# A fused attention and MoE kernel whose first half is put into one written order of small pieces

## The chip, the cores and the metric

The kernel runs on one core of a Trainium2 chip. The time is device microseconds of one execution; lower is better. The kernel before took 707.45 us (median of three runs, 704.58 to 709.62). The profiled execution took 706.18 us, and the span of its trace, from its first to its last instruction, is 704.4 us. "PE" is the engine of the matrix multiplications, "DVE" the vector engine, "ACT" the scalar engine, "POOL" GpSimd and "SP" the engine that issues nearly all transfers.

## The reference

```python
scale = 1.0 / np.sqrt(D)                      # B, H, S, Ns, D = 8, 8, 512, 32, 64
scores = scale * np.matmul(x, state.transpose(0, 1, 3, 2))
a = softmax(scores)                           # over the 32 states
xread = np.matmul(a, state)
scores2 = scale * np.matmul(state, x.transpose(0, 1, 3, 2))
a2 = softmax(scores2)                         # over the 512 tokens
sread = np.matmul(a2, x)
y = np.concatenate([xread, sread], axis=2)    # 8 x 8 x 544 x 64 -> 4352 tokens x 512
h = np.maximum(y @ w_in, 0.0)                 # w_in 512 x 2048
out = h * h @ w_out                           # w_out 2048 x 512
```

Here `softmax` stands for the subtraction of the maximum, the exponential and the division by the sum. `w_in` and `w_out` arrive as 64-bit floats and are decoded to 32 bits on the chip.

## The kernel before

**What is computed in which form.** For a batch, `xread @ w_in` is `a @ (state @ w_in)`, so the kernel makes a small matrix W2 = state @ w_in for each batch (256 rows of heads and states by 2048) and multiplies the attention weights by that. The weights of the second matrix stay as they are. Products are done in two parts: every operand X is split into a rounded `hi` and a rest `lo`, and a product is hi*hi + hi*lo + lo*hi (`mm3`, L303).

**Blocks and chunks.** There are nine blocks of tokens: the 512 token rows of each of the eight batches, and a ninth of the 256 rows of `sread` of all batches. The 2048 columns of `w_in` are cut into 16 chunks of 128, called fc. `hidden.b.fc` (L638) makes the chunk of the hidden layer: six multiplications 128x512 into a tile `ph`, a square of the positive part on ACT alone (L651, L652, keys under `square` in SECOND) or on ACT and DVE (L655, L656), a `g_hi` on ACT (L657) and a `g_lo` on DVE (L662). `accumulate.b.fc` (L665) multiplies it by `w_out` into four tiles `acc`, twelve multiplications for a batch. Batches 0 and 1 are interwoven over the first 16 chunks, and their sums are stored after four and eight chunks (`keep_first`, `keep_part`) so that both can share the decoded chunks of `w_out`.

**Preparing a batch.** `start`, `load` and `prep` bring x and transpose it (L382; for batches 0 and 1 by PE with `ident`, L394, and copies on DVE or ACT, for later ones on DVE, L388). `scores` multiplies by the states. The softmax over states transposes the scores on DVE (`transposed_scores`, L409), takes the maximum, the difference, the exponential, the sum and the quotient (L434 to L451), transposes back on DVE (L449) and splits into `k_hi` and `k_lo`. `exp_s` (L412) is the softmax over tokens; `transposes` and `sread` finish it.

**Preparing weights.** `load_raw` brings a piece of `w_in` (512 KB), `decode_wi` decodes it (L316: an absolute value on ACT, a clamp on DVE or POOL, three bit operations on DVE) and writes it to memory. `prep_wo` does the same for a chunk of `w_out` and splits it (L631). `direct_w2.hb` makes W2 for batches 0 and 1 and 256 columns, `later_w2.hb.2` and `later_w2.hb.4` for batches 2 to 5, `last_w2` for 6 and 7; before the later ones `load_wf` reads the decoded `w_in` back (512 KB, L541). The results of the later ones go to memory (L584) and come back by `load_w2` (L613), which splits them on ACT and on DVE or POOL (L621, L279).

**What sets the order.** PLAN (L24) lists these steps in order. The program calls them one after another, but each engine's own order is then set by a scheduler that moves instructions by estimated times. Only instructions under `keep_in_program_order` stay: from `hidden.2.8` on (PINNED_FROM) those of PE, the loads of `w_out`, and those named under `pin` in SECOND. SECOND (L188) also says which engine does an operation that two could do. Each engine runs its instructions strictly in its order, and SP issues transfers strictly in its own. PSUM holds four `acc` tiles, two `ph` tiles and two `psb` tiles for all the rest (L253 to L255).

Of the kernel before, what the change touches and what calls it, by code (L numbers as in the profile page):

```python
# [23 lines left out]
PLAN = """  # L24
    load_raw.0 ident neg_ident start.0 load.0.1 load_states.0 load_raw.1 states.0 decode_wi.0 prep.0.0
        load_raw.2 load_wo.0 decode_wi.1 direct_w2.0 prep_wo.0 load_wo.1 decode_wi.2 start.1 load.1.1
    prep_wo.1 load_raw.3 decode_wi.3 prep.0.1 scores.0 transposed_scores.0.1 softmax.0.1 exp_s.0.1
# [3 lines left out]
    prep_wo.3 softmax.1.0 softmax.1.1 load_wo.4 accumulate.0.0
    exp_s.1.0 exp_s.1.1 direct_w2.1 hidden.0.2 hidden.0.3 transposes.0 sread.0 load_wo.5 accumulate.0.1
    hidden.1.0 decode_wi.4 load_raw.6 decode_wi.5 load_raw.7 direct_w2.2 load_wo.6 load_wo.7 accumulate.0.2
    hidden.1.1 transposes.1 prep_wo.4 decode_wi.6 load_raw.8 decode_wi.7 direct_w2.3 load_raw.9
        accumulate.0.3
    hidden.1.2 prep_wo.5 sread.1 accumulate.1.0
    hidden.1.3 prep_wo.6 prep_wo.7 load_wo.8 load_wo.9 accumulate.1.1
# [16 lines left out]
    hidden.0.13 softmax.2.0 load_n.2.0 load_part.0 accumulate.0.11
    hidden.0.14 later_w2.3.2 later_w2.3.4 load_wf.1.4 later_w2.4.2 load_w2.1.5 later_w2.4.4 accumulate.0.12
    hidden.0.15 softmax.2.1 load_n.2.1 accumulate.0.13
    hidden.1.8 transposes.2 accumulate.0.14
    hidden.1.9 load_wf.1.5 load_w2.1.6 accumulate.0.15
    hidden.1.10 sread.2 accumulate.1.8
    hidden.1.11 later_w2.5.2 later_w2.5.4 load_wf.1.6 load_w2.1.7 accumulate.1.9  # L60
    hidden.1.12 start.3 load_part.1 accumulate.1.10
# [834 lines left out]
```

## Time and profile before

| | |
|---|---|
| time of the profiled execution | 706.18 us |
| span of its trace | 704.4 us |
| median of the runs | 707.45 us |
| busy: PE, DVE, ACT, POOL | 660.6, 375.3, 334.7, 78.2 us |
| moved by transfers | 100.36 MB, 142 GB/s |
| mean granted clock of PE | 0.991 |

How to read it: an engine's busy time is the union of its instructions' spans, so a PE that is busy may still run slower than it could. A view of windows gives each engine's busy time in stretches of the span, with the number of instructions in brackets behind an x. A group line gives line, engine, operation, output<-input by tile names with their numbers left out, shapes and types, the count, then busy time and the mean of one in nanoseconds, then the idle time just before these instructions and what ended it. A line of the view of waits says who waited for whom, for how long in all, how often and at most. Lines of a timeline begin with the start and the length in us.

### The profile page before, as it was taken

How to read it: one execution, taken by the hardware profiler on the slowest of the kernel's cores; microseconds unless marked ns; L12 is line 12 of the kernel's file. 1: busy time of each engine (PE TensorE's matmuls, PEld its weight loads, DVE VectorE, ACT ScalarE, POOL GpSimd, SP SyncE). 2: the span in 40 equal slices, each digit the busy share in tenths (PEclk: the TensorE clock that was granted, in tenths of full speed). 3: DMA queues.
4: the chain of work that ended last, by engine and by line, in shares of the span. 5: the costliest groups of instructions: out<-in, count | busy, mean ns of one | idle time of the engine just before them, and what ended most of it. 6: DMA issues, size and time to landing. Idle time of an engine off the chain costs nothing.

```text
span 704.4 us, 11391 instructions
## 1 busy us (share of the span) xinstructions
PE 660.6 (94%) x4365; PEld 512.0 (73%) x4365; DVE 375.3 (53%) x691; ACT 334.7 (48%) x643; POOL 78.2 (11%) x66
## 2 busy tenths in 40 slices
PE   4668899979989999999999999999999999999997
PEld 1445666657667777887788778877887788888885
DVE  4999988667444448244924382438332733433232
ACT  2657765365623436434634464445444544444322
POOL 0302021013200003000300021002100200100000
PEclk9989999999999999999999999999999999999999
DMA  9556577895588775333533353433432223230003
GB/s 231 128 208 187 174 235 273 192 371 175 186 247 237 207 217 163 76 106 121 176 72 108 121 174 70 116 104 97 143 120 76 86 79 120 60 91 30 31 1 89
DMA packets 120710, 100.36 MB, mean 142 GB/s; under 512 B 68048, under 2 KB 96976, under 8 KB 120656
## 3 DMA queue, kind: packets, MB, share of 16 engines
q1 hardware_dynamic: 120512, 99.51, 47.8%
q8 instruction: 34, 0.56, 0.3%
q10 hardware_dynamic: 144, 0.13, 0.1%
q14 instruction: 20, 0.16, 0.1%
HBM read 65.54 MB, written 34.08 MB: 141 GB/s over the span
## 4 chain that ended last, share of the span: by engine, by line
PE 71%; DVE 9%; DMA 9%; SPq 4%; ACT 3%; issue 2%; POOL 0%; DVEq 0%; ACTq 0%
PE acc L309 43%; PE ph L309 22%; DMA wi_raw<-in_moe_w_in_dram 3%; SPq L376 2%; DMA w_d<-w2o 2%; DMA wo_raw<-in_moe_w_out_dram 2%; PE w2ps L341 1%; PE w2ps L338 1%; PE pt L472 1%; DVE wf L329 1%; DMA xp<-in_x_dram 1%; PE st L338 1%; DMA win_f<-wf 1%; DMA wf<-win_f 1%; DVE wf L330 1%
## 5 line engine op out<-in xcount | busy, mean ns | idle before, releaser
L309 PE MATMUL acc<-wo,g_hi 128*128 128x512 f32 x1086 | 338.6, 397 | 8.0 <-ACT wo L278 3.0
L309 PEld LDWEIGHTS acc<-wo,g_hi 128*128 128x128 f32 x1086 | 202.1, 190 | 62.1 <-issue 4.5
L309 PE MATMUL acc<-wo,g_lo 128*128 128x512 f32 x543 | 208.0, 392 | 0.0
L309 PE MATMUL ph<-k_hi,w 128*128 128x512 f32 x512 | 180.8, 395 | 5.8 <-DVE g_lo L662 2.7
L662 DVE TENSOR_TENSOR g_lo<-ph,g_hi 128x512 fp32r<-128x512 f32 (+1 forms) x140 | 91.4, 655 | 135.8 <-ACT g_hi L657 133.8
L309 PEld LDWEIGHTS ph<-k_hi,w 128*128 128x128 f32 x512 | 96.3, 189 | 31.6 <-DVE g_lo L662 4.9
L309 PEld LDWEIGHTS acc<-wo,g_lo 128*128 128x128 f32 x543 | 102.4, 189 | 23.1 <-issue 1.2
L657 ACT CAST g_hi<-ph 128x512 fp32r<-128x512 f32 (+1 forms) x144 | 81.2, 565 | 49.7 <-DVE ph L656 42.4
L309 PE MATMUL ph<-k_lo,w 128*128 128x512 f32 x256 | 100.6, 393 | 0.1
L655 ACT ACTIVATE r<-ph 128x512 f32<-128x512 f32 (+1 forms) x77 | 43.7, 568 | 107.3 <-PE ph L309 107.0
L656 DVE SCALAR_TENSOR_TENSOR ph<-ph,r 128x512 f32<-128x512 f32 (+1 forms) x77 | 50.6, 657 | 82.8 <-ACT r L655 82.5
L651 ACT ACTIVATE ph<-ph 128x512 f32<-128x512 f32 (+1 forms) x67 | 38.0, 567 | 98.1 <-PE ph L309 98.1
L309 PEld LDWEIGHTS ph<-k_lo,w 128*128 128x128 f32 x256 | 48.4, 189 | 10.5 <-DVE k_lo L279 0.5
L279 POOL TENSOR_TENSOR w<-w_f,w 128x512 fp32r<-128x512 f32 x18 | 24.1, 1339 | 283.4 <-ACT w L278 283.4
L652 ACT ACTIVATE ph<-ph 128x512 f32<-128x512 f32 (+1 forms) x67 | 38.1, 569 | 1.4
L341 PE MATMUL w2ps<-wf,sT 64*32 64x256 f32 x960 | 35.8, 390 | 0.7 <-ACT srd L494 0.7
L278 ACT CAST w<-w_f 128x512 fp32r<-128x512 f32 x40 | 24.5, 614 | 5.0 <-DMA w_f<-w_d 5.0
L388 DVE STREAM_TRANSPOSE xT<-xp 128x512 f32<-128x512 f32 x24 | 16.0, 693 | 18.7 <-PE st L341 9.5
L338 PE MATMUL w2ps<-wf,sT 64*32 64x256 f32 x64 | 20.1, 395 | 5.9 <-DVE wf L330 4.0
L309 PE MATMUL ph<-sr_hi,s 128*128 128x256 f32 x128 | 25.5, 282 | 0.0
L279 POOL TENSOR_TENSOR s<-sf,s 128x512 fp32r<-128x512 f32 x8 | 10.3, 1292 | 128.8 <-ACT s L278 128.8
L309 PEld LDWEIGHTS ph<-sr_hi,s 128*128 128x128 f32 x128 | 21.0, 191 | 0.6
(94 smaller groups left out, 557.3 us busy)
## 6 DMA issues: line engine op xcount, KB each, us to landing
w_d<-w2o SPq DMA_DIRECT2D x40, 256.0 KB, 4.5
w_f<-w_d SPq DMA_DIRECT2D x40, 256.0 KB, 3.1
wi_raw<-in_moe_w_in_dram SPq DMA_DIRECT2D x16, 512.0 KB, 5.1
wo_raw<-in_moe_w_out_dram SPq DMA_DIRECT2D x16, 512.0 KB, 6.4
wf<-win_f SPq DMA_DIRECT2D x16, 512.0 KB, 4.3
w<-w2a_d SPq DMA_DIRECT2D x16, 512.0 KB, 3.3
out_dram<-o SPq DMA_DIRECT2D x31, 256.0 KB, 3.0
xp<-in_x_dram SPq DMA_DIRECT2D x96, 64.0 KB, 2.8
```

Source lines behind the costliest of these rows:

```text
L278: nc.scalar.copy(hi, src)
L279: pick(key, nc.gpsimd, nc.vector).tensor_sub(lo, src, hi.bitcast(F32))
L309: m = nc.tensor.matmul(ps, l, r, start=first and i == 0, stop=last and i == len(seq) - 1, skip_group_check=skip)
L338: in_order(call())
L341: tc.keep_in_program_order(call())
L388: nc.vector.transpose(xT[:, c], self.xp[g][:, c])
L651: nc.scalar.activation(ph, ph, AF.Relu)
L652: nc.scalar.activation(ph, ph, AF.Square)
L655: nc.scalar.activation(r, ph, AF.Relu)
L656: nc.vector.scalar_tensor_tensor(ph, ph, 0.0, r, ALU.max, ALU.mult)
L657: nc.scalar.copy(ghi, ph)
L662: nc.vector.tensor_sub(glo, ph, ghi.bitcast(F32))
```

## The change

The change rewrites the order of the work up to the fourth batch and a few operations with it.

- Every engine's instructions up to `hidden.3.0` (LOOSE_FROM) are kept in program order, by a wrapper around the engines (`InOrder`). The scheduler moves none of them. From there on PLAN and the scheduler are as before, but for `load_wf.2.3`.
- Steps are generators with a `yield` between their instructions. A name in PLAN that is repeated runs one piece of its step each time, so PLAN orders single instructions. `accumulate` of batches 0 and 1 now does all `hi` products first and, as a piece of its own, the `lo` products.
- The softmax over states of batches 0 and 1 is done from PE transposes: `keep_s` copies the scores on ACT to SBUF, PE transposes them into PSUM (`pst`), DVE takes maximum and difference from there, PE transposes the result back (`pa`), and the split reads that. x of these batches is loaded in rows of 1 KB and loaded again later (`load_n`, tile `xr`) for `sread`; `exp_s` of these batches comes later.
- For the first 512 of the 2048 columns (`hb` 0 and 1, NOW = 2) W2 of all eight batches is made in a row from the decoded `w_in` while it is still in SBUF, and four of the sixteen reads `load_wf` are gone. The products of `hb` 0 for batches 2 to 7 use the two `ph` tiles.
- SECOND moves operations between engines. Over the whole program, in counts: squares on ACT alone 62 to 81 (those shared with DVE 66 to 47, chunks of 512 tokens); copies of W2 out of PSUM on DVE 16 to 7; splits of `w_out` on POOL 7 to 13; clamps on POOL 2 to 8; corrections on PE (`neg_ident`, L293) 10 to 4.

Lines of the changed kernel below are those of its own file; nearly all its instructions are issued on line 317, so tile names tell them apart.

```diff
 PLAN = """
-    hidden.0.1 prep_wo.2 prep.1.0 prep.1.1 scores.1 transposed_scores.1.0 load_raw.5 transposed_scores.1.1
-        load_raw.4
+    hidden.0.1 hidden.0.1 hidden.0.1 accumulate.0.0 second_w2.1 hidden.0.1 hidden.0.1 softmax.1.0 prep_wo.1
+        prep_wo.1 hidden.0.1 softmax.1.1 softmax.1.1 softmax.1.1 prep_wo.1 prep_wo.1 softmax.1.0 softmax.1.0
...
+LOOSE_FROM = "hidden.3.0"
 PINNED_FROM = "hidden.2.8"
...
+class InOrder:
+    def __init__(self, engine, tc, held):
+        self.engine, self.tc, self.held = engine, tc, held
+    def __getattr__(self, name):
+        call = getattr(self.engine, name)
+        def issue(*args, **kw):
+            op = call(*args, **kw)
+            if self.held:
+                self.tc.keep_in_program_order(op)
+            return op
+        return issue
...
-    nc = tc.nc
+    held = ["start"]
+    nc = Engines(tc.nc, tc, held)
...
         def transposed_scores(self, g):
             b = self.b
+            if b < NT:
+                pool, tag = (ps_acc, "acc") if b == 0 else (ps_b, "psb")
+                self.sp[g] = pool.tile([P, S], F32, tag=tag, name=f"pst{b}_{g}")
+                for k in range(KC):
+                    nc.tensor.transpose(self.sp[g][:, ts(k, P)], self.e_all[:, g, ts(k, P)], ident)
+                return
...
+            if b < NT:
+                pool, tag = (ps_acc, "acc") if b == 0 else (ps_b, "psb")
+                pa = pool.tile([P, S], F32, tag=tag, name=f"pa{b}_{g}")
+                for k in range(KC):
+                    nc.tensor.transpose(pa[:, ts(k, P)], sp[:, ts(k, P)], ident)
+                yield
+                nc.scalar.copy(khi[:, g], pa)
+                yield
+                nc.vector.tensor_sub(klo[:, g], pa, khi[:, g].bitcast(F32))
+                return
...
     def two_w2(hb, b0, last):
         w = (wf.pop(hb) if last else wf[hb]).bitcast(F32)
-        ps = [ps_b.tile([P, 2, HB], F32, tag="psb", name=f"w2ps{hb}_{b0}_{g}") for g in range(G)]
+        pool, tag = (ps_h, "ph") if hb == 0 < b0 else (ps_b, "psb")
+        ps = [pool.tile([P, 2, HB], F32, tag=tag, name=f"w2ps{hb}_{b0}_{g}") for g in range(G)]
...
     def direct_w2(hb):
-        ps = two_w2(hb, 0, True)
+        ps = two_w2(hb, 0, hb >= NOW)
...
     def later_w2(hb, b0):
-        keep_w2(hb, b0, two_w2(hb, b0, b0 == 4))
+        yield from keep_w2(hb, b0, two_w2(hb, b0, b0 == 4 and hb >= NOW))
...
         ghi, glo = g
+        if blk < NX:
+            for i in range(nt // P):
+                for r in range(2):
+                    nc.tensor.matmul(acc[i], ghi[:, ts(i, P)], wo[fc][:, r], start=first and r == 0, stop=False)
+            yield
+            for i in range(nt // P):
+                nc.tensor.matmul(acc[i], glo[:, ts(i, P)], wo[fc][:, 0], start=False, stop=last)
+            return
...
+        if begun[k] is None or left[k] == 0:
+            for _ in begun[k] or ():
+                pass
+            done.add(k)
+        else:
+            next(begun[k], None)
```

**Two places where the instructions move.** On DVE, behind the first batch's softmax and ahead of its first `g_lo`. Before (`dec` and `wf` are pieces of `w_out` and `w_in` being decoded, `nb2`, `s2` and `r2` are small tiles of `exp_s` of batch 0, `xT1` is x of batch 1):

```order
L430 TENSOR_SCALAR r20_1_283<-s20_1_281 128x1
L329 SCALAR_TENSOR_TENSOR dec0_191<-wo_raw0_154,dec0_191 128x512
L431 RECIPROCAL r20_1_283<-r20_1_283 128x1
L323 TENSOR_SCALAR wf1_202<-wf1_202 128x512
L330 SCALAR_TENSOR_TENSOR dec0_191<-wo_raw0_154,dec0_191 128x512
...
L430 TENSOR_SCALAR r20_0_308<-s20_0_306 128x1
L326 TENSOR_SCALAR wf1_202<-wf1_202 128x512 x2
L431 RECIPROCAL r20_0_308<-r20_0_308 128x1
L329 SCALAR_TENSOR_TENSOR wf1_202<-wi_raw3_230,wf1_202 128x512
L329 SCALAR_TENSOR_TENSOR wf1_202<-wi_raw2_152,wf1_202 128x512
L287 COPY xT1_1_364<-px1_1_1_371 128x512
```

In the changed kernel (`pst1` and `pa0` are PE's transposes for batches 1 and 0, `m11` the maxima):

```order
L317 TENSOR_TENSOR k_lo0_120<-pa0_0_330,k_hi0_119 128x512
L317 TENSOR_TENSOR k_lo0_120<-pa0_1_337,k_hi0_119 128x512
L317 TENSOR_SCALAR dec0_328<-dec0_328 128x512
L317 TENSOR_SCALAR wf1_242<-wf1_242 128x512
L317 SCALAR_TENSOR_TENSOR dec0_328<-wo_raw0_182,dec0_328 128x512
...
L317 SCALAR_TENSOR_TENSOR wf1_242<-wi_raw3_244,wf1_242 128x512
L317 TENSOR_REDUCE m11_1_422<-pst1_1_410 128x16
...
L317 TENSOR_TENSOR sp1_1_421<-pst1_1_410,m11_1_422 128x512
```

The small operations of `exp_s` and the copies of `xT1` have left this stretch of DVE, and batch 1's softmax stands directly behind batch 0's.

On SP, where the loads for the second half of the first 16 chunks stand. Before (`w2_d` is W2 in memory, written from `w2o`; `w2_f` is its reload; `wi_raw` and `wo_raw` are raw weights, `win_f` the decoded `w_in`):

```order
L628 DMA wo_raw11_1068<-in_moe_w_out_dram 128x1024
L537 DMA win_f6_83<-wf6_1105 128x512
L525 DMA wi_raw14_1112<-in_moe_w_in_dram 128x2x512
L620 DMA w2_f0_4_1206<-w2_d4_89 128x512
L628 DMA wo_raw12_1210<-in_moe_w_out_dram 128x1024
L537 DMA win_f6_83<-wf6_1105 128x512
L525 DMA wi_raw15_1146<-in_moe_w_in_dram 128x2x512
```

In the changed kernel:

```order
L317 DMA wo_raw8_1020<-in_moe_w_out_dram 128x1024
L317 DMA w2_d4_89<-w2o4_0_0_1055 128x2x256
L317 DMA wi_raw11_1118<-in_moe_w_in_dram 128x2x512
L317 DMA w2_d4_89<-w2o4_0_1_1094 128x2x256
L317 DMA win_f5_82<-wf5_1018 128x512
L317 DMA win_f6_83<-wf6_1078 128x512
L317 DMA wi_raw13_1143<-in_moe_w_in_dram 128x2x512
L317 DMA wo_raw10_1147<-in_moe_w_out_dram 128x1024
L317 DMA part_d0_101<-po0_0_1167 128x512
L317 DMA part_d0_101<-po0_1_1170 128x512
L317 DMA w2_f0_4_1177<-w2_d4_89 128x512
```

Raw pieces of `w_in` now stand later in the queue beside the reload of W2: pieces 11 and 13 where 14 and 15 stood, each behind writes of results that ACT or DVE must first have made.

More of the change, by code (lines that the diff above doesn't have):

```diff
@@ L31 @@
[L31 to L37, printed above, removed]
@@ L54 @@
[L54 to L61, printed above, removed]
@@ new lines @@
+    hidden.2.10 accumulate.2.9 load_n.2.1 transposes.2 transposes.2 hidden.2.10 hidden.2.10 hidden.2.10
+        load_w2.3.1 transposes.2 transposes.2 hidden.2.10 softmax.3.0 load_n.2.0
+    hidden.2.11 hidden.2.11 load_w2.2.6 hidden.2.11 hidden.2.11 hidden.2.10 load_w2.3.1 hidden.2.11
+        hidden.2.11 load_w2.2.7 later_w2.5.4 load_w2.2.7 later_w2.5.4 load_w2.2.7 accumulate.2.10
+        softmax.3.0 load_wf.2.2 sread.2 sread.2 sread.2 later_w2.5.4 sread.2 sread.2
+    hidden.2.12 later_w2.5.4 hidden.2.12 hidden.2.12
@@ new lines @@
+    hidden.2.13 hidden.2.12 hidden.2.12 hidden.2.12 exp_s.3.1 later_w2.5.4 exp_s.3.0 transposes.3
+        transposes.3 transposes.3 transposes.3 load_w2.3.0 accumulate.1.15 load_n.3.0 hidden.2.13
+        hidden.2.13 hidden.2.13 hidden.2.13 hidden.2.13 softmax.3.0 softmax.3.0 accumulate.2.11 load_w2.3.0
+        softmax.3.0 softmax.3.0 softmax.3.0 softmax.3.0
+    hidden.2.14 load_n.3.1
+    hidden.2.15 hidden.2.15 hidden.2.15 hidden.2.15 hidden.2.15 hidden.2.15 later_w2.7.4 later_w2.7.4
+        later_w2.7.4 later_w2.7.4 accumulate.2.12 load_w2.3.1 hidden.2.14 hidden.2.14 hidden.2.14
+        hidden.2.14 load_w2.3.0 hidden.2.14 later_w2.7.4 sread.3 sread.3 sread.3 accumulate.2.13 sread.3
+        sread.3
@@ L620, in load_w2 @@
         nc.sync.dma_start(raw, w2_d[hb][b])
-        split(*weights[b, hb], raw, f"w2_lo.{b}.{hb}")
+        yield
+        yield from split(*weights[b, hb], raw, f"w2_lo.{b}.{hb}")
     wo = {}
@@ L752, in step_hidden @@
             ks[blk] = att[blk].k
-        gs[blk, fc] = hidden(blk, fc, tok[blk])
+        yield from hidden(blk, fc, tok[blk])
     def step_accumulate(blk, fc):
@@ L799, in tile_attn_moe @@
             key("sread", b), lambda b: att[b].sread(), b,
-            after=[key("transposes", b)] + [key("load_n", b, g) for g in range(G)] * (not early),
+            after=[key("transposes", b)] + [key("load_n", b, g) for g in range(G)],
         )
@@ L855, in tile_attn_moe @@
             step(key("accumulate", blk, fc), step_accumulate, blk, fc, after=needs)
[L857 to L859 removed]
+    plan = PLAN.split()
+    left = {k: plan.count(k) for k in steps}
+    done, begun = set(), {}
+    for k in plan:
+        if k == LOOSE_FROM:
+            held.clear()
         if k == PINNED_FROM:
             pinned.append(k)
[L862 to L864 removed]
+        if k not in begun:
+            f, args, after = steps[k]
+            assert done.issuperset(after), f"{k} needs {set(after) - done}"
+            begun[k] = f(*args)
+        left[k] -= 1
+        if begun[k] is None or left[k] == 0:
+            for _ in begun[k] or ():
+                pass
+            done.add(k)
+        else:
+            next(begun[k], None)
     assert done == set(steps), set(steps) - done
```

452 lines of the change are left out of this document (317 added, 135 removed), and 3 rows, old and new, of the table SECOND.

## The prediction

> **What bounds the kernel now.** I read the slices of the page first.
>
> ```profile
> span 704.4 us, 11391 instructions
> PE   4668899979989999999999999999999999999997
> DVE  4999988667444448244924382438332733433232
> ```
>
> PE is full from about the tenth slice of 17.6 us on; before that it isn't, and DVE is full just there. To see the stretches, I cut the span at four instructions of PE: the first multiplication of `hidden.0.0`, `hidden.0.4`, `hidden.0.12` and `hidden.3.0`, found by counting `ph` multiplications in the order (288 without the corrections stand before the last).
>
> ```profile
> 26.38 1.22 PE L309 MATMUL ph<-k_hi,w 128*128 128x512 f32 x2 [0.42 <-ACT k_hi L278]
> 87.02 0.39 PE L309 MATMUL ph<-k_hi,w 128*128 128x512 f32 x1
> 154.15 0.39 PE L309 MATMUL ph<-k_hi,w 128*128 128x512 f32 x1
> 299.29 0.39 PE L309 MATMUL ph<-k_hi,w 128*128 128x512 f32 x1
> ```
>
> ```profile
> core 0: us, PE busy (x) PEld busy (x) DVE busy (x) ACT busy (x) POOL busy (x), PEclk, DMA share, GB/s
> 0.00:26.40 26.40, 11.51 (x74) 5.01 (x74) 16.43 (x33) 8.86 (x17) 4.26 (x9) 1.00 1.02 233
> 26.40:87.00 60.60, 48.03 (x391) 33.17 (x392) 58.35 (x123) 41.42 (x87) 9.64 (x7) 0.92 0.49 164
> 87.00:154.10 67.10, 59.32 (x467) 42.87 (x467) 48.22 (x85) 35.97 (x68) 8.61 (x5) 1.00 0.84 264
> 154.10:299.30 145.20, 142.57 (x1138) 105.41 (x1138) 78.04 (x142) 69.04 (x130) 19.49 (x16) 1.00 0.66 192
> 299.30:704.40 405.10, 399.22 (x2300) 325.49 (x2298) 174.26 (x313) 179.43 (x343) 36.16 (x29) 1.00 0.32 95
> ```
>
> From 26.4 to 87.0 us DVE is busy 58.35 of 60.6 us (96%), and hardly ever waits:
>
> ```profile
> DVE r L430 <- ACT e L421: 1.0, 1, 1.0
> DVE wf L323 <- ACT wf L322: 0.7, 1, 0.7
> DVE w L577 <- ACT w L572: 0.3, 1, 0.3
> ```
>
> So this stretch is DVE's. The next is mixed: no engine is full, and the transfers are at 0.84. From 154 us on PE sets the time (142.57 of 145.2, then 399.22 of 405.1), and no order of the others can shorten that by more than its few idle microseconds. The change has its room ahead of 154 us.
>
> **The end, from `hidden.3.0`.** PLAN and scheduler are the same but for one read. I take 405.1 us as it is. With the 1.8 us that the execution (706.18) is longer than its span, the sum needs only the time of `hidden.3.0`, now 299.3.
>
> **What leaves DVE.**
>
> ```profile
> L656 DVE SCALAR_TENSOR_TENSOR ph<-ph,r 128x512 f32<-128x512 f32 x66 | 45.8, 695 | 67.2 <-ACT r L655 66.9
> L287 DVE COPY w2o<-w2ps 128x512 f32<-128x512 f32 x16 | 10.8, 680 | 4.2 <-PE w2ps L341 4.1
> L279 DVE TENSOR_TENSOR wo<-dec,wo 128x512 fp32r<-128x512 f32 x9 | 6.3, 705 | 1.4 <-ACT wo L278 1.3
> L409 DVE STREAM_TRANSPOSE sp<-st 128x512 f32<-128x512 f32 x16 | 11.1, 700 | 3.6 <-PE st L341 3.6
> L655 ACT ACTIVATE r<-ph 128x512 f32<-128x512 f32 x66 | 39.5, 599 | 89.2 <-PE ph L309 89.0
> L652 ACT ACTIVATE ph<-ph 128x512 f32<-128x512 f32 x62 | 36.3, 585 | 1.2
> ```
>
> Nineteen squares fewer (19 x 0.695 = 13.2 us), nine copies of W2 (6.1), six splits of `w_out` (4.2) and eight transposes of the softmax (5.6) are 29 us; smaller moves in both directions roughly cancel. On ACT the squares cost 19 x (2 x 0.585 - 0.599) = 10.9 us. The copies of W2 and the four `keep_s` are thirteen more operations of that length, 7.6 us. ACT has the room: it is busy 41.42 of 60.6 us where DVE is full.
>
> What the sum needs is how much stands ahead of `hidden.0.12`. Now DVE has run 33 + 123 + 85 = 241 instructions by then, 123.0 us, 0.510 us each. In the new order 205 stand ahead of that chunk's `g_lo`: `exp_s`, `transposes` and `sread` of batches 0 and 1 come later too. 205 x 0.510 = 104.6 us.
>
> **What POOL takes on.**
>
> ```profile
> L446 POOL TENSOR_TENSOR sp<-sp,s 128x512 f32<-128x512 f32 x11 | 12.3, 1122 | 47.4 <-DVE s L445 46.9 <-PE ph L309 0.5
> L279 POOL TENSOR_TENSOR wo<-dec,wo 128x512 fp32r<-128x512 f32 x7 | 9.8, 1396 | 38.4 <-ACT wo L278 36.5 <-PE ph L309 1.9
> L323 POOL TENSOR_SCALAR wf<-wf 128x512 f32<-128x512 f32 x2 | 4.3, 2156 | 5.2 <-DMA win_f<-wf 3.8 <-ACT wf L322 1.4
> ```
>
> Ahead of `hidden.0.12` the order has 8 clamps (8 x 2.156), 10 splits of `w_out` (10 x 1.396), 3 products of the softmax (3 x 1.122) and a split of about 1.4 us: 36 us where POOL now has 4.26 + 9.64 + 8.61 = 22.5. It stays far from full. A clamp on POOL is a wait added for DVE: the shift of the same piece stands in DVE's queue, with the rest of that queue behind it. On DVE an operation of that size takes 0.42 us (row L326 below), on POOL 2.156, so eight exposed clamps would cost 8 x 1.7 = 14 us. The order puts other pieces of DVE's work ahead of the shift (between the clamp of `dec0` and its shift, batch 0's last products and `k_lo`), and I count nothing, with 14 us as the bound. But DVE's decoding is slower beside POOL:
>
> ```profile
> 31.68 1.40 POOL L279 TENSOR_TENSOR wo<-dec,wo 128x512 fp32r<-128x512 f32 x1 [3.99 <-ACT wo L278]
> 31.95 1.68 DVE L329 SCALAR_TENSOR_TENSOR wf<-wi_raw,wf 128x512 uint32<-128x512 uint32 x1
> L329 DVE SCALAR_TENSOR_TENSOR wf<-wi_raw,wf 128x512 uint32<-128x512 uint32 x16 | 11.8, 745 | 0.2
> L330 DVE SCALAR_TENSOR_TENSOR wf<-wi_raw,wf 128x512 uint32<-128x512 uint32 x16 | 10.8, 682 | 0.2
> L326 DVE TENSOR_SCALAR wf<-wf 128x512 uint32<-128x512 uint32 x16 | 8.5, 537 | 0.8 <-POOL wf L323 0.6
> L326 DVE TENSOR_SCALAR dec<-dec 128x512 uint32<-128x512 uint32 x16 | 6.7, 419 | 0.1
> ```
>
> The one at 31.95 took 1.68 us instead of 0.68. POOL's 13.5 us more are about ten instructions; the bounds are 0 and ten times 1.0 us. The means show 16 x (0.063 + 0.118) = 2.9 us over these two kinds, so I take 3 us. [...]
>
> **What PE gains and loses.**
>
> ```profile
> 300.81 2.72 PE acc L309 x12
> 278.05 1.09 PE pt L472 x8
> 91.90 0.40 PE L338 MATMUL w2ps<-wf,sT 64*32 64x256 f32 x1
> 92.92 0.50 PE L293 MATMUL ph<-g_hi,neg_ident 128*128 128x512 f32 x1
> 85.85 1.01 PE L341 MATMUL pr<-xn,eT 128*32 128x64 f32 x59
> ```
>
> A large multiplication is 0.227 us in a row, a transpose 0.136, a W2 product of two batches (91.90 to 92.92) 1.02. The transposes of two softmaxes are 32 x 0.136 = 4.4 us more, six corrections fewer about 1.4 us less: 3.0 us more in all. Ahead of `hidden.0.12` the order also has 16 more `acc` (3.6) and three more W2 products (3.1), and 64 `pr` (about 2.0) and 8 `pt` (1.1) fewer: 6.6 us more done. So `hidden.0.12` to `hidden.3.0` keeps 145.2 - (6.6 - 3.0) = 141.6 us.
>
> **When `hidden.0.12` comes.** DVE stands idle 154.1 - 123.0 = 31.1 us ahead of it. Keeping every idle microsecond, DVE gives 104.6 + 3 + 31.1 = 138.7. PE, with its 118.9 busy us, 6.6 more, and only the idle 14.9 us ahead of 26.4, gives 140.4. The lower end is DVE at its 96% behind 26.4: 26.4 + (107.6 - 16.4) / 0.963 = 121. The upper end is 154 (nothing gained), or beyond it (the slower rival). The new order brings DVE, ACT and PE close together, so each will wait for the others at times; I take the side where the idle time stays, **140**.
>
> Sum: 140 + 141.6 + 405.1 + 1.8 = **688.5 us**, 17.7 under the profiled execution; on the median of the runs, 1.3 us higher, it would be 689.8.
>
> **Edits costed at nothing.** Four reads fewer:
>
> ```profile
> PE w2ps L338 <- DMA wf<-win_f: 1.6, 3, 1.1
> ```
>
> PE waits 1.6 us in all for such reads, so no more than that can come of them directly. Fewer and larger pieces of x: transfers are at 1.02 in the first 26.4 us, so if they stayed as long, `hidden.0.0` would come no earlier; the sum doesn't use it. The W2 products of `hb` 0 in the `ph` tiles stand ahead of `hidden.0.1`, which must wait until ACT and DVE have emptied them (two copies of 0.59 us a pair, the length of the ACT operations above): covered by the softmax of batch 1, which needs those engines anyway; 3 x 1.2 us if that cover is gone.
>
> The clock row is 0.92 between 26.4 and 87.0 us: 0.08 x 60.6 = 4.8 us of full speed lost. [...]
>
> **The rivals.** (a) *A larger gain.* PE and DVE really interlock: `hidden.0.12` at 128, between 121 and 140, giving 676.5. For it: DVE waits 2.0 us in 60 now. Against: three engines near their limit. (b) *Transfers keep the date.* `hidden.0.12` needs W2 that was loaded, decoded, multiplied, written and read back, and the share of 0.84 shows a busy queue; SP's new order puts raw pieces behind writes. Then it stays at 154.1, only 3.6 us of PE's work are saved: 702.6. Against: the share is 0.49 up to 87 us, 30 us to spare. (c) *Slower: loads hold ACT.*
>
> ```profile
> ACT wf L322 <- DMA wi_raw<-in_moe_w_in_dram: 17.9, 10, 3.1
> ACT dec L322 <- DMA wo_raw<-in_moe_w_out_dram: 13.3, 9, 4.5
> ```
>
> ACT's 178 instructions ahead of `hidden.0.12`, at (8.86 + 41.42 + 35.97) / 172 = 0.501 us, are 89 us, with 5 us for the first load 94. Thirty-one of them open a decoding and wait for a load, with squares queued behind, and PE waits for those. At the 1.64 us that a wait has now, that is 145 in all, near the forecast. From 2.05 us on (157.7) the gain is gone. At 2.5 us, half as long again, it is 171.7, and the kernel takes 720.2.
>
> **How the numbers follow.** Chances: forecast 0.48 (own range 681 to 697), (a) 0.22, (b) 0.16, (c) 0.14. A measurement can tell about 1% here, 7 us. Forecast and (a) are faster by more, with a little of (b): 0.72; same 0.14; slower 0.14. The range from 670 to 708 leaves out (c) and the far end of (a).
>
> **What would show it.** `hidden.0.12` near 140 and `hidden.3.0` near 282, with the 405 us behind it unchanged; some 205 DVE instructions ahead of the former; DVE no longer at 96% up to 87 us. The prediction is wrong if ACT's waits for loads grow past 60 us, if the stretch behind `hidden.3.0` changes by more than 3 us, or if PE is cut up by short waits all over the first 150 us.

## The result, and the profile after

The changed kernel takes **682.02 us** (median of 4 runs, 680.75 to 684.21) where the kernel before took 707.87 beside it (4 runs, 704.58 to 709.62): a ratio of 0.9643, with a 95% interval from 0.96 to 0.9687. Forecast were 688.5 us, range 670 to 708. The profiled execution took 684.21 us, its span 682.3.

The slices of the page, as they answer to those of before:

```profile
span 682.3 us, 11470 instructions
PE   4899997999999997999999999999999999999997
DVE  5899997877433445438443743465234614323232
PEclk9899999999999999899999999999999999999999
```

PE is now full from the third slice on (17.1 us each), but for the 7th and the 16th, and DVE is still full in slices 3 to 6. The same four first multiplications cut the span (in the third row two are printed together, and the chunk's own is the second, at 133.3):

```profile
26.07 0.50 PE L317 MATMUL ph<-k_hi,w 128*128 128x512 f32 x1
66.11 0.47 PE L317 MATMUL ph<-k_hi,w 128*128 128x512 f32 x1
133.10 0.62 PE L317 MATMUL ph<-k_hi,w 128*128 128x512 f32 x2
277.29 0.39 PE L317 MATMUL ph<-k_hi,w 128*128 128x512 f32 x1
```

`hidden.0.4` comes at 66.1 instead of 87.0 us, `hidden.0.12` at 133.3 instead of 154.1, `hidden.3.0` at 277.3 instead of 299.3. So 20.9 of the 22.0 us are won ahead of `hidden.0.4`; the stretch from there to `hidden.0.12` takes 67.2 us as it took 67.1, and the end 405.0 instead of 405.1. Busy time by stretch, after:

```profile
core 0: us, PE busy (x) PEld busy (x) DVE busy (x) ACT busy (x) POOL busy (x), PEclk, DMA share, GB/s
0.00:26.10 26.10, 15.36 (x212) 11.64 (x212) 15.80 (x29) 14.80 (x30) 5.58 (x9) 0.93 0.93 285
26.10:66.10 40.00, 38.87 (x336) 26.90 (x330) 38.76 (x71) 33.23 (x66) 13.19 (x9) 1.00 0.78 249
66.10:133.30 67.20, 61.69 (x424) 46.48 (x425) 57.95 (x104) 44.12 (x83) 15.22 (x10) 0.97 0.83 253
133.30:277.30 144.00, 139.48 (x1162) 105.81 (x1161) 74.69 (x135) 79.91 (x152) 24.62 (x20) 0.98 0.60 176
277.30:682.30 405.00, 399.18 (x2300) 325.54 (x2298) 174.07 (x312) 179.40 (x343) 36.16 (x29) 1.00 0.34 101
```

Read DVE's column against the one of before. Up to `hidden.0.4` it was busy 16.43 + 58.35 = 74.8 us and idle 12.2; now it is busy 15.80 + 38.76 = 54.6 and idle 11.5. Its idle time has hardly changed: the 20.9 us are 20.2 us of DVE's work that no longer stand there. Half of that has not gone away. In the next stretch DVE does 57.95 us instead of 48.22, and that stretch is no longer for it, since DVE was idle 18.9 us there and now only 9.2.

The loads that hold ACT (rival c) were 31.2 us of waits before; now, up to `hidden.0.12`:

```profile
ACT wf L317 <- DMA wi_raw<-in_moe_w_in_dram: 6.9, 5, 2.5
ACT dec L317 <- DMA wo_raw<-in_moe_w_out_dram: 1.1, 2, 0.6
```

Two single waits behind a reloaded W2 remain, the first two rows on ACT, the third PE's wait behind the second of them:

```profile
115.85 0.62 ACT L317 CAST w<-w_f 128x512 fp32r<-128x512 f32 x1 [4.47 <-DMA w_f<-w_d]
268.43 0.62 ACT L317 CAST w<-w_f 128x512 fp32r<-128x512 f32 x1 [1.93 <-DMA w_f<-w_d]
270.69 1.94 PE L317 MATMUL pr<-xr,eT 128*32 128x64 f32 x64 [4.17 <-ACT w2o L317]
```

What made the first load late is in SP's queue: its read of W2 waits for the write of W2, and that stands behind eight reads of x which take SP 8.08 us. The second read of W2 stands directly behind eight more (the last two rows).

```profile
99.20 8.08 SPq L317 DMA_DIRECT2D xp<-in_x_dram  x8
108.52 0.40 SPq L317 DMA_DIRECT2D w_d<-w2o  x1
111.95 0.33 SPq L317 DMA_DIRECT2D w_f<-w_d  x1
...
257.07 7.71 SPq L317 DMA_DIRECT2D xp<-in_x_dram  x8
264.88 0.57 SPq L317 DMA_DIRECT2D w_f<-w_d  x1
```

### The profile page after: what moved, and what is told of

It is laid out like the page before. It is cut to its first block, busy times and chain, and to the rows that moved or that the text cites. A ratio compares the mean times of both kernels' runs of the same rounds, so it can differ in the third digit from the quotient of the medians.

```text
span 682.3 us, 11470 instructions
## 1 busy us (share of the span) xinstructions
PE 654.6 (96%) x4423; PEld 516.4 (76%) x4423; DVE 361.3 (53%) x648; ACT 351.5 (52%) x672; POOL 94.8 (14%) x76
## 4 chain that ended last, share of the span: by engine, by line
PE 73%; DVE 13%; DMA 7%; ACT 4%; issue 2%; SPq 1%; POOL 0%; DVEq 0%; ACTq 0%; POOLq 0%
PE acc L317 44%; PE ph L317 22%; DVE wf L317 3%; PE w2ps L317 2%; DVE dec L317 2%; DMA xn<-in_x_dram 2%; DMA w_f<-w_d 2%; DVE g_lo L317 2%; PE pr L317 1%; DVE s L317 1%; DMA w_d<-w2o 1%; DMA wi_raw<-in_moe_w_in_dram 1%; PE st L317 1%; DVE sp L317 1%; DVE m L317 1%
## 5 line engine op out<-in xcount | busy, mean ns | idle before, releaser
L317 PE MATMUL acc<-wo,g_hi 128*128 128x512 f32 x1090 | 326.1, 395 | 0.0
L317 PE MATMUL acc<-wo,g_lo 128*128 128x512 f32 x545 | 197.8, 392 | 0.5 <-DVE g_lo L317 0.3
L317 ACT ACTIVATE ph<-ph 128x512 f32<-128x512 f32 (+1 forms) x172 | 98.4, 572 | 104.1 <-PE ph L317 101.7
L317 ACT ACTIVATE r<-ph 128x512 f32<-128x512 f32 (+1 forms) x58 | 32.3, 558 | 90.9 <-PE ph L317 90.8
L317 DVE SCALAR_TENSOR_TENSOR ph<-ph,r 128x512 f32<-128x512 f32 (+1 forms) x58 | 37.4, 644 | 73.1 <-ACT r L317 72.9
L317 POOL TENSOR_TENSOR w<-w_f,w 128x512 fp32r<-128x512 f32 x21 | 27.3, 1303 | 205.9 <-ACT w L317 202.7
L317 POOL TENSOR_TENSOR s<-sf,s 128x512 fp32r<-128x512 f32 x8 | 10.3, 1292 | 128.8 <-ACT s L317 128.8
L317 PE MATMUL w2ps<-wf,sT 64*32 64x256 f32 x768 | 26.9, 382 | 0.1
L317 DVE SCALAR_TENSOR_TENSOR wf<-wi_raw,wf 128x512 uint32<-128x512 uint32 x32 | 25.4, 795 | 0.9
L317 ACT COPY w2o<-w2ps 128x512 f32<-128x512 f32 x33 | 18.7, 591 | 12.6 <-PE w2ps L317 11.4
L317 DVE SCALAR_TENSOR_TENSOR dec<-wo_raw,dec 128x512 uint32<-128x512 uint32 x32 | 24.1, 754 | 0.6
```

Of the source, the lines that this page charges most:

```text
L317: op = call(*args, **kw)
```

## The experiments

My theory at the outset: DVE's amount of work sets the time up to `hidden.0.12`, and the work that left it makes the gain. The rival: the written order makes it. Each kernel ran on the same chip as the kernel before, beside it (705.93 to 707.87 us in the median there), and the ratio is to that. Dates are those of the profiled execution (which took 5.3 us more than the median for e7, 3.3 for e10, and within 2.3 of it for the others); "DVE" is its busy and its idle time ahead of `hidden.0.4`.

| kernel | median us | ratio to before (95%) | 0.4 | 0.12 | 3.0 | DVE to 0.4 |
|---|---|---|---|---|---|---|
| before | 707.87 | 1 | 87.0 | 154.1 | 299.3 | 74.8 + 12.2 |
| after | 682.02 | 0.9643 (0.96 to 0.9687) | 66.1 | 133.3 | 277.3 | 54.6 + 11.5 |
| e1_free_order | 713.19 | 1.0096 (1.0065 to 1.0126) | 93.9 | 159.0 | 304.5 | 64.8 + 29.1 |
| e2_squares_back | 688.96 | 0.9752 (0.9705 to 0.9799) | 68.7 | 134.7 | 282.3 | 56.0 + 12.7 |
| e3_new_sides_old_order | 726.78 | 1.0293 (1.0248 to 1.0338) | 85.5 | 158.3 | 316.8 | 70.5 + 15.0 |
| e4_two_stalls | 679.41 | 0.9624 (0.9577 to 0.9672) | 66.0 | 131.1 | 268.2 | 54.8 + 11.2 |
| e5_old_sides | 731.29 | 1.0315 (1.0266 to 1.0364) | 92.2 | 171.7 | 324.5 | 65.5 + 26.7 |
| e6_x4_early | 676.13 | 0.9548 (0.951 to 0.9587) | 68.5 | 133.1 | 270.3 | 54.7 + 13.8 |
| e7_hold_dve_act | 696.74 | 0.9863 (0.9816 to 0.991) | 76.5 | 146.4 | 293.5 | 56.5 + 20.0 |
| e8_hold_pe_sp | 721.99 | 1.0202 (1.0167 to 1.0236) | 93.3 | 165.1 | 314.2 | 61.7 + 31.6 |
| e9_held_to_0_4 | 703.43 | 0.9946 (0.9925 to 0.9966) | 71.4 | 149.5 | 297.6 | 59.4 + 12.0 |
| e10_dve_pad | 689.56 | 0.9766 (0.9736 to 0.9796) | 72.9 | 142.5 | 285.9 | 60.7 + 12.2 |
| e11_act_pad | 681.95 | 0.965 (0.9628 to 0.9673) | 65.2 | 131.4 | 275.7 | 54.8 + 10.4 |
| e12_clamps_back | 684.17 | 0.9692 (0.966 to 0.9725) | 66.8 | 133.5 | 277.3 | 55.1 + 11.7 |

### e1_free_order: the same operations without the written order

```diff
-LOOSE_FROM = "hidden.3.0"
+LOOSE_FROM = "load_raw.0"
```

> The changed kernel with all its operations and sides, but LOOSE_FROM is its first step, so that nothing is held and the scheduler places every instruction, as it did before the change. My theory: the gain comes from the work that has left DVE (some 29 us) and the written order only lets it be used; then the scheduler, with the same amounts on the same engines, keeps most of it: hidden.0.12 by 141 us and 682 to 690 us in all. Rival: the gain is made by the written order, since the scheduler orders by modelled durations and the loads land later than modelled; then hidden.0.12 falls back to 150 us or later and the kernel takes 697 to 708 us.

The rival is right, and beyond its range: 713.19 us, 1.0% slower than before the change. The loss, 27.2 us at `hidden.3.0`, has all arisen by `hidden.0.4` (27.8). Its first stretch, and ACT's and DVE's waits in it:

```profile
0.00:93.90 93.90, 69.10 (x559) 45.83 (x560) 64.83 (x124) 55.30 (x108) 25.54 (x22) 0.87 0.62 198
```

```profile
ACT wf L317 <- DMA wi_raw<-in_moe_w_in_dram: 9.8, 6, 4.9
ACT wo L317 <- DVE dec L317: 7.1, 4, 2.9
ACT dec L317 <- DMA wo_raw<-in_moe_w_out_dram: 4.5, 2, 3.5
ACT dec L317 <- POOL wo L317: 3.1, 4, 1.2
```

```profile
DVE wf L317 <- ACT wf L317: 6.8, 2, 5.3
DVE r L317 <- ACT e L317: 5.2, 1, 5.2
DVE g_lo L317 <- ACT g_hi L317: 4.4, 3, 2.3
DVE m L317 <- ACT e L317: 3.8, 1, 3.8
```

The scheduler does two things that the written order doesn't. It puts 124 DVE instructions ahead of `hidden.0.4` instead of 99 or 100 (10.3 us more), and it puts instructions at the head of ACT's queue whose input is not there: ACT waits 14.3 us for loads (4.5 in the changed kernel), 7.1 for DVE's decoding (0.9) and 3.1 for POOL (none), and DVE then stands idle 29.1 us instead of 11.5. (Of the rows of DVE's waits, the first was there before: 5.5 us in the changed kernel; the other three are not in its list.) Why the scheduler chose so, the rival's modelled durations, was not tried.

### e2_squares_back, e3_new_sides_old_order, e5_old_sides: the sides

In e2 the `square` row of SECOND is the one of before, in e3 the kernel before has the whole new table, in e5 the changed kernel has the whole old one. The table has the `pin` row too, so that e3 also changes what the scheduler may not move: `decode_wi.3` and `decode_wi.8` are pinned in addition, `decode_wo.2`, `exp_s.0.0` and `exp_s.0.1` no longer. Of e2's diff the first line:

```diff
-    square: 0.0 0.1 0.2 0.3 0.4 0.6 0.7 0.8 0.9 0.10 0.11 0.12 0.13 0.14 0.15 1.0 1.1 1.2 1.3 1.4 1.5 1.6
...
+    square: 0.0 0.1 0.2 0.3 0.4 0.6 0.7 0.9 0.10 0.11 0.12 0.13 1.1 1.3 1.6 1.8 1.10 2.0 2.2 2.3 2.6 2.9
```

> The changed kernel with the squares on the sides that they had before: twenty go back from ACT to DVE and ACT together, one goes to ACT. Everything else, the written order too, stays. Six of the twenty stand ahead of hidden.0.12 (6 x 0.695 = 4.2 us of DVE), thirteen net behind it. My theory (DVE's amount of work sets the date up to hidden.0.12, PE from there on): hidden.0.12 comes 3 to 5 us later, near 137 us, the stretch from there to hidden.3.0 stays within 1.5 us of 144, and the kernel takes 685 to 688 us. Rival (DVE has room in the written order, and ACT, which the squares load twice, was no worse off): hidden.0.12 stays within 1 us of 133.3 and the kernel within 1.5 us of 682.

The total lies 1 us above what I had expected of my theory, but not where I had put it: `hidden.0.12` is only 1.4 us later, and 3.4 of the 5.0 us at `hidden.3.0` arise in batch 2 (193.5 to 282.3, 88.8 us, against 191.9 to 277.3, 85.4). DVE is far from full there. What is different in the rows is that PE, full from 191.9 to 251.9 us in the changed kernel, has gaps in two of the same three pieces of 20 us here (18.70 and 19.72 busy). They make 1.6 of the 3.4 us; PE's busy time in batch 2 is another 1.6 us longer (82.84 instead of 81.23). A square by DVE sends a chunk to ACT, DVE, ACT and DVE again instead of ACT and DVE; that this longer way makes the gaps is argued from the order, not shown.

> The kernel before the change with the new table of sides (SECOND) and nothing else: its own plan, the scheduler's order, softmax of all batches by DVE's transposes. Ahead of hidden.0.12 about 15 us leave DVE (six squares 4.2, some five copies of W2 3.4, six splits of w_out 4.2, eight clamps 3.4). My theory by DVE relief: hidden.0.12 comes 8 to 14 us earlier, 140 to 146, and the kernel takes 693 to 700 us. Rival (sides alone are worth nothing without the order): within 3 us of 707, since ACT's and POOL's waits take the place of what DVE saves.

Neither: the new sides without the new order cost 21 us against the kernel before beside them (705.93). DVE's 4.3 us of relief ahead of `hidden.0.4` are there (70.45 instead of 74.78), but `hidden.0.12` comes at 158.3 and the stretch behind it takes 158.5 us instead of 145.2.

> The changed kernel in its written order with the table of sides (SECOND) of before. The first four kernels have turned my theory over: the same operations and sides under the scheduler take 713 us, and the new sides in the old order 727. New theory: the written order makes the gain, and the sides pay only in it. Then with the old sides the order alone keeps most: about 22 squares, copies and splits return to DVE ahead of hidden.0.12 (some 15 us less what waits hide), hidden.0.12 between 140 and 148, 690 to 698 us in all. Rival (order and sides were made for each other, neither is worth anything alone): 703 us or more, no better than before the change.

The rival, and beyond it: 731.29 us. The order with the old sides leaves DVE idle 26.7 us ahead of `hidden.0.4`. Where the old sides have an operation on another engine, the head of the next engine's queue waits for it, as I read these rows (in the changed kernel the first is 5.5 us, the last 1.3, and the other two are not in the lists):

```profile
DVE wf L314 <- ACT wf L314: 8.4, 3, 5.4
DVE ph L314 <- ACT r L314: 5.5, 1, 5.5
```

```profile
ACT ph L314 <- PE ph L314: 8.0, 4, 5.1
ACT w2o L314 <- PE w2ps L314: 4.0, 2, 2.6
```

So everything but the sides costs 24 us and the sides, with their pins, 21, and together they gain 26: this order and these sides were made for each other. An order fit for the old sides was not tried, and e5 holds the other edits too (the PE transposes, the early W2), so 24 us is not the order's price alone. With e1 and e3 my theory, as I had stated it, has fallen: the relief of DVE makes no gain by itself.

### e7_hold_dve_act, e8_hold_pe_sp, e9_held_to_0_4: which part of the order

In e7 only DVE and ACT are held, in e8 only PE and SP, with the other pair in the second line; in e9 `LOOSE_FROM` is `"hidden.0.4"`.

```diff
-            if self.held:
+            if self.held and self.kept:
...
-            setattr(self, name, InOrder(getattr(nc, name), tc, held))
+            setattr(self, name, InOrder(getattr(nc, name), tc, held, name in ('vector', 'scalar')))
```

> The changed kernel with the written order kept on DVE and ACT alone; PE, POOL and SP are placed by the scheduler. Theory A (the gain is the order on the two engines that are near full ahead of hidden.0.4: no instruction that waits for a late transfer stands ahead of ready ones): hidden.0.4 by 72 us, 682 to 692 us in all. Theory B (it is PE's and SP's order, what is read and multiplied first): 700 us or more.

> The counterpart: the written order kept on PE and SP alone; DVE, ACT and POOL are placed by the scheduler. Theory A (the order of DVE and ACT makes the gain): 700 us or more, hidden.0.4 later than 85 us. Theory B (PE's and SP's order makes it): hidden.0.4 by 72 us, 682 to 692 us in all. If both of these come near 682, either order leads the scheduler to the other; if both come near 710, only the order of all engines together makes the gain.

e8 is clear: with PE and SP alone held, DVE is idle 31.6 us ahead of `hidden.0.4`, and the kernel is slower than with nothing held. e7 lies between the two theories: `hidden.0.4` at 76.5, 10.5 of the 20.9 us, and 696.74 in all. Against the kernel with nothing held (e1) DVE's and ACT's order alone gains 16 us; another 15 come only when PE, POOL and SP are held with them, although PE's and SP's order alone loses 9. Against the kernel before, e7 is worth about 10 us of 26.

> The changed kernel with the written order kept only up to hidden.0.4; from there on the scheduler places everything. In e1_free_order the whole loss stood ahead of hidden.0.4 (27.8 us there, 27.2 at hidden.3.0). Theory (what the written order is worth, it is worth in the first 66 us): hidden.0.4 within 2 us of 66, from there to hidden.3.0 210 to 215 us as in all the other kernels, 681 to 687 us in all. Rival (the order is worth as much behind hidden.0.4, and the scheduler loses there what it gets early): hidden.0.4 to hidden.3.0 over 220 us, 692 us or more.

The rival. From `hidden.0.4` to `hidden.3.0` it takes 226.2 us instead of 211.2, and `hidden.0.4` itself is 5.3 us late, since the scheduler slips 15 DVE instructions of later steps in ahead of it (114 instead of 99). Work that was put off is still to be done: the scheduler, with some 9 us of DVE's work more behind `hidden.0.4` than before the change (56.93 instead of 48.22), doesn't fit it into DVE's idle time as the written order does (78.1 us to `hidden.0.12` instead of 67.2).

```profile
71.40:149.50 78.10, 65.25 (x418) 46.32 (x417) 56.93 (x101) 42.62 (x81) 16.98 (x11) 0.91 0.81 248
```

### e10_dve_pad, e11_act_pad: is DVE full, and has ACT room?

Ten operations of 128x512 that nobody needs are put at ten places between `hidden.0.0` and `hidden.0.4`; e11 has `nc.scalar.copy(srall[:, 2:], srall[:, :2])` there.

```diff
+    def pad():
+        nc.gpsimd.memset(srall[:, :2], 1.0)
+        for _ in range(10):
+            yield
+            nc.vector.tensor_sub(srall[:, 2:], srall[:, :2], srall[:, :2])
+
+    step("pad", pad)
```

> The changed kernel with ten subtractions of 128x512 (0.6 to 0.7 us each) added to DVE's written order, evenly between hidden.0.0 and hidden.0.4; they write to a tile that holds nothing yet, so no other engine waits for their results. They add 6 to 7 us to DVE. Theory (DVE, busy 38.76 of 40.0 us there, sets the time of this stretch): hidden.0.4 5.5 to 7 us later, at 71.6 to 73, and 4 to 7 us more in all, 686 to 689. Rival (PE, busy 38.87 us of the same 40.0, sets it, and DVE's work can slide into the next stretch, where it has 9 us of room): hidden.0.4 within 2 us of 66, 682 to 684 in all.

> The same with ten copies of 128x512 (0.5 to 0.6 us each) on ACT at the same places. Theory (ACT has 6.8 us of 40 left, so that squares and copies could go to it): hidden.0.4 at most 2.5 us later, and 682 to 685 us in all. Rival (in a written order each instruction that is put into a queue delays all behind it, whatever room the engine has): hidden.0.4 5 to 6 us later and 687 us or more, as much as the same work costs on DVE.

The added groups (count, then shortest, median and longest in ns), and the stretch up to `hidden.0.4`, first on DVE, then on ACT:

```profile
L317 DVE TENSOR_TENSOR srall<-srall x10: 679/681/687, 30.1 to 76.5; 128x512 f32<-128x512 f32 x10
```

```profile
0.00:72.90 72.90, 57.59 (x540) 38.68 (x540) 60.69 (x108) 47.89 (x94) 19.57 (x19) 0.98 0.75 236
```

```profile
L317 ACT COPY srall<-srall x10: 611/619/676, 26.5 to 65.8; 128x512 f32<-128x512 f32 x10
```

```profile
0.00:65.20 65.20, 54.96 (x540) 37.29 (x541) 54.76 (x101) 51.86 (x103) 19.25 (x19) 1.00 0.85 266
```

Nine of the ten on DVE run ahead of `hidden.0.4` (108 instructions instead of 99): 9 x 0.681 is 6.1 us, just what DVE's busy time has gained (60.69 against 54.56), and `hidden.0.4` comes 6.8 us later, the median 7.5. Ten times 0.619 us on ACT move nothing: 681.95 us. So within the written order the first half of my theory stands: DVE's work is the time there, and ACT has room for what it took over. PE is busy 38.87 of the same 40.0 us; whether ten operations more on PE would cost as much was not tried, so DVE need not be the only bound.

### e12_clamps_back: POOL beside DVE

```diff
-    decode_wi: 2 6 8
-    decode_wo: 0 1 6 12 14
```

> The changed kernel with the eight clamps (three of W_in, five of w_out) on DVE again instead of POOL. DVE gets 8 x 0.42 = 3.4 us more ahead of hidden.0.12; POOL loses some 16 us there, beside which DVE's decoding operations take 1.1 to 1.2 us instead of 0.69. Theory (what DVE saves by a clamp on POOL it loses again by the contention): 680 to 684 us, no difference. First rival (only DVE's count of operations matters): 3 to 4 us later at hidden.0.12 and 685 us or more. Second rival (clamps on POOL cost more than they save, since shifts wait behind them): 679 us or less.

No difference that can be told (684.17 us, intervals overlapping; the same dates within 0.7 us). Up to `hidden.0.12` POOL is busy 18.6 us instead of 34.0, and DVE 114.0 instead of 112.5: eight clamps of 0.42 us are 3.4, and a transpose of x (0.68) has slipped behind the cut, so 2.7 more were due and 1.5 came. Some 1.2 us thus come back by less contention, about a third of what the clamps cost, and the rest has gone into DVE's idle time (20.8 to 19.5 us): the forecast of no difference was met, but not by the reason given for it alone. A difference of 2 us in the total is below what these runs can tell. How POOL weighs on DVE is seen in the changed kernel: one operation of POOL, the clamp and shift of a decoding beside it on DVE (102.13), and the same pair with POOL idle (106.55).

```profile
102.16 1.53 POOL L317 TENSOR_TENSOR w<-w_f,w 128x512 fp32r<-128x512 f32 x1 [16.34 <-ACT w L317]
```

```profile
102.13 1.85 DVE L317 TENSOR_SCALAR wf<-wf 128x512 f32<-128x512 f32 x2
...
106.55 0.88 DVE L317 TENSOR_SCALAR dec<-dec 128x512 f32<-128x512 f32 x2
```

### e4_two_stalls, e6_x4_early: the two waits that were left

e4 issues the reads of x for batch 2 in two halves and holds the order up to `hidden.3.2`. e6 adds that the reads for batch 4 stand earlier and the order is held up to `hidden.3.4`. The edits of e6, which hold those of e4:

```diff
         accumulate.1.6 hidden.0.8 hidden.0.8 prep_wo.10 prep_wo.10 prep_wo.10 direct_w2.6 load_wf.1.2
+        start.2
...
-    hidden.2.14 load_n.3.1
+    hidden.2.14 load_n.3.1 start.4
...
-    hidden.3.0 start.4 accumulate.2.14
+    hidden.3.0 accumulate.2.14
...
-LOOSE_FROM = "hidden.3.0"
+LOOSE_FROM = "hidden.3.4"
...
+                yield
...
-        att[b].load(0)
+        yield from att[b].load(0)
```

> The changed kernel with two edits against its two longest waits of PE behind a reloaded W2: the eight reads of x for batch 2 (start.2, 8.1 us on SP's queue) are issued in two halves, the second half behind the read of W2 of hb 5, and the order is held up to hidden.3.2 instead of hidden.3.0, so that load_w2.3.2 and the reads of x for batch 4 no longer get in ahead of the end of batch 2. My theory (those two waits are what kept hidden.0.12 to hidden.3.0 at 144.0 us instead of the 141.6 that was forecast): PE's waits of 2.7 us at 116.5 and 4.2 us at 270.7 go, with the half clock behind them; hidden.0.12 1 to 3 us earlier, hidden.3.0 4 to 9 us earlier, 673 to 678 us in all. Rival (another wait of the same size follows, since the loads are only one of several inputs that PE lacks there): less than 2 us gained, 680 to 683.

```profile
131.10:268.20 137.10, 136.67 (x1161) 103.67 (x1160) 72.12 (x130) 79.26 (x151) 24.41 (x20) 1.00 0.56 174
268.20:677.80 409.60, 401.12 (x2300) 326.61 (x2299) 177.09 (x317) 179.72 (x344) 36.12 (x29) 0.99 0.36 103
```

Both theories have a part, and the total, 679.41 us, can't be told from the changed kernel's by the two ratios. The waits are gone and `hidden.3.0` is 9.1 us earlier, but 4.6 us are lost again right behind it, in a wait that was not there: the scheduler puts batch 4's transposes of x into DVE's queue ahead of batch 3's products, and with the order held longer those reads come later.

```profile
270.10 0.71 DVE L318 STREAM_TRANSPOSE xT<-xp 128x512 f32<-128x512 f32 x1 [3.35 <-DMA xp<-in_x_dram]
273.67 0.71 DVE L318 STREAM_TRANSPOSE xT<-xp 128x512 f32<-128x512 f32 x1 [2.27 <-DMA xp<-in_x_dram]
276.55 0.71 DVE L318 STREAM_TRANSPOSE xT<-xp 128x512 f32<-128x512 f32 x1 [1.59 <-DMA xp<-in_x_dram]
```

> The two edits of e4_two_stalls with two more against the wait that was seen to follow there (DVE stood 7.2 us behind the reads of x for batch 4, and PE 2.6 us behind DVE): the reads start.4 stand ahead of hidden.2.14, where the scheduler had put them, and the order is held up to hidden.3.4, so that the transposes of batch 4 stand behind the products of batch 3's first chunks. Theory (that stretch is a matter of what stands in a queue ahead of a late read): hidden.3.0 stays near 268, the stretch behind it goes back from 409.6 to 405 us, 672 to 676 us in all. Rival (the wait moves once more): 677 us or more.

As the theory said, with 676.13 us a shade above its range: from `hidden.3.0` on it takes 406.0 us again. (That `hidden.3.0` itself is 2.1 us later than in e4 comes from the start: `hidden.0.4` was 2.5 us later already, and PE waited 10.1 us for the first reads of x in this execution, 7.4 in e4.)

```profile
133.10:270.30 137.20, 136.70 (x1161) 103.68 (x1160) 71.21 (x130) 79.17 (x151) 24.96 (x20) 1.00 0.58 176
270.30:676.30 406.00, 399.49 (x2300) 325.45 (x2298) 177.02 (x317) 180.75 (x344) 36.22 (x29) 1.00 0.36 103
```

This version beats both kernels: 4.5% under the one before, and 1.0% under the changed one by the two ratios, whose intervals don't meet.

## Why the prediction was right, and where it was wrong

**The bound** was right: DVE ahead of `hidden.0.4`, PE from batch 0's last quarter on, and the stretch behind `hidden.3.0` unchanged (405.0). e10 and e11 show the first directly, though not that DVE alone is the bound there.

**The forecast of `hidden.0.12`** (140, measured 133.3) was made of a count, a length and an idle time. The count was right (29 + 71 + 104 = 204, forecast 205). The length was not: 112.5 us busy, 0.551 each instead of 0.510, so 104.6 + 3 was 4.9 us short. The mean of before was not fit for the new mix: of its operations 24 in 239 were shorter than 0.3 us, of those that stand there now 10 in 202, and DVE's spans overlap less (they add up to 137.9 us before, with 123.0 busy, and to 122.5 now, with 112.5; both sums are estimates from the group means). What failed most is the step "I take the side where the idle time stays". DVE's idle time went from 31.1 to 20.8 us: it stayed ahead of `hidden.0.4` (12.2 to 11.5), where there was none to take, and halved behind it (18.9 to 9.2), because the order brings work there from the full stretch. 112.5 + 20.8 is 133.3. The other side of the sum, PE with 118.9 + 6.6 busy and 14.9 idle, failed too: PE was busy 115.9 us and idle 17.4. Most of that is in one stretch: between `hidden.0.0` and `hidden.0.4` the multiplications of `acc` and `ph` took 38.4 us before (122 of them) and take 31.1 now (121), at a clock row of 0.92 then and 1.00 now, so busy time was no fixed amount of work. That both wrong sides gave nearly the same, 138.7 and 140.4, was chance. The prediction looked at one sum up to `hidden.0.12` and missed that DVE was full in the first half of it and had room in the second, though its own windows showed that.

**"29 us leave DVE"** was right for the four kinds named, but the other moves don't cancel. The first rows of the page, before and after:

```profile
PE 660.6 (94%) x4365; PEld 512.0 (73%) x4365; DVE 375.3 (53%) x691; ACT 334.7 (48%) x643; POOL 78.2 (11%) x66
```

```profile
PE 654.6 (96%) x4423; PEld 516.4 (76%) x4423; DVE 361.3 (53%) x648; ACT 351.5 (52%) x672; POOL 94.8 (14%) x76
```

Net, DVE lost 14.0 us, 13.8 of them ahead of `hidden.3.0` and 10.5 ahead of `hidden.0.12` (123.0 to 112.5). Of the 20.2 us that left the time ahead of `hidden.0.4`, 9.7 are thus only put off, and it is the written order that puts them off. What the PE transposes of the softmax and the early W2 of all batches are worth by themselves was not tried apart.

**POOL's contention** was about the size that I took, 3 us, from the group means of before. After, the groups of decoding operations with two inputs read, over the whole program,

```profile
L317 DVE SCALAR_TENSOR_TENSOR wf<-wi_raw,wf 128x512 uint32<-128x512 uint32 x32 | 25.4, 795 | 0.9
L317 DVE SCALAR_TENSOR_TENSOR dec<-wo_raw,dec 128x512 uint32<-128x512 uint32 x32 | 24.1, 754 | 0.6
```

and ahead of `hidden.0.12` all 110 decoding operations add up to 68.9 us, where the group means of before would give 66.1: 2.8 us more. So most of the 4.9 us by which DVE's time is above the forecast belong to the mean of 0.510 and not to POOL (four small `s` operations of the softmax add 1.1 us: 0.448 us each instead of 0.162). e12 puts what the contention takes back of the clamps' saving at about a third. The 14 us that eight exposed clamps could have cost did not appear: DVE waits 0.3 us in all from 26.1 to 66.1 us.

```profile
DVE wf L317 <- ACT wf L317: 0.3, 1, 0.3
```

This row and 38.76 us of 40.0 show that "DVE no longer at 96% up to 87 us" was wrong: it is at 97% up to 66 us. The stretch has become shorter, not easier.

**`hidden.0.12` to `hidden.3.0`** was to take 141.6 us and took 144.0, and it is near by two errors that nearly cancel. e4 and e6 run as many instructions of PE there, to within one, in 137.1 and 137.2 us, so the forecast was 4.4 us too long for the work; and the wait at 270.7 us with the slow multiplications behind it (0.63 us instead of 0.39, up to 276 us), which the sum didn't have, cost some 6.8 by that difference.

**The clock.** The row is 1.00 from 26.1 to 66.1 us where it was 0.92. But the 4.8 us of full speed lost, the prediction's estimate from that row, are not a gain by themselves: DVE set that stretch, and the clock was lost elsewhere (0.93 instead of 1.00 up to 26.1 us, 0.97 and 0.98 instead of 1.00 in the two stretches behind 66.1). Over the whole span it is 0.990 where it was 0.991; in the other three executions of the changed kernel it was 0.994 to 0.997. Behind the two single waits for a reloaded W2 the row of the changed kernel is 0.50: from 116.6 to 119.5 us behind PE's wait of 2.72 us, and from 270.7 to 276.0 us behind the one of 4.17. In e4, by the rows of the last section, multiplications of the same 0.63 us stand behind a gap of 2.61 us.

**The rivals.** (a) foresaw 676.5 us, and with `hidden.0.12` at 133.3, between it and the forecast, it was half right. (b) fell: the transfers keep no date. (c), loads that hold ACT, did not happen (8.0 us of waits up to `hidden.0.12`, where the kernel before had 31.2). The scheduler's order of the same operations (e1) doesn't bring the growth that (c) needs either: its waits of this kind are 14.3 us up to `hidden.0.4`, more than the 4.5 of the changed kernel but less than the 17.4 of the kernel before. Of a similar kind are the two single waits for a reloaded W2, which (c) didn't name; e6, without them, is 6 us faster.

**What the prediction did not see** is that order and sides are worth less than nothing apart. It priced the change as work that leaves an engine, as if the order were only the way to use it. By e3 the new sides alone take 727 us. The forecast came out because the order was fit for the sides, which I had assumed, not argued: as far as that goes, it was luck.

## What to carry to other kernels

Cut the time ahead of a milestone into busy and idle time of the bounding engine, stretch by stretch: where it is full, only less work or work put off helps, and work put off is free at most as far as the engine is idle in the next stretch (in e9 it was not free). A table of engine sides and an order of the queues are one design; here, with one of them changed alone, the queues got heads that wait. Ten idle operations put on an engine tell in one run whether its work is on the path; an engine that is as full beside it needs a run of its own.

## What the runs showed of the hardware

Behind a gap on PE of 2.61 us the multiplications took 0.63 us instead of 0.39 (e4; the last row is from behind the slow piece):

```profile
280.54 1.00 PE L318 MATMUL acc<-wo,g_hi 128*128 128x512 f32 x2 [2.61 <-DVE o L318]
281.34 0.63 PE L318 MATMUL acc<-wo,g_lo 128*128 128x512 f32 x1
...
284.96 0.39 PE L318 MATMUL ph<-k_hi,w 128*128 128x512 f32 x1
```

Operations of DVE with one SBUF input were slower beside POOL too: the two at 102.13 us above took 1.85 us together, the two at 106.55 only 0.88. Over the first 134 us of the changed kernel, decoding operations that overlap one of POOL's by over 0.2 us take 0.74 us instead of 0.43 with one input, and 0.96 instead of 0.70 with two (means from the timelines). And the strided reads of x cost SP's queue between 0.67 us each (eight in 5.37 us, at 172.0) and 1.0 (eight in 8.08 us) against 0.40 for the write and 0.33 and 0.57 for the reads of W2 in the rows above, so that eight of them delay what stands behind by 5 to 8 us.
